# Storing a second MLP's weights already split, spacing that work out, and starting the second MLP inside the last block of the first

## The chip, the cores and the metric

The kernel runs on one NeuronCore of one Trainium2 chip. The metric is device time in microseconds, the median of three runs. Besides it there is one profiled execution, from which every number of the trace comes. The engines are PE (matrix products), ACT, DVE and POOL (elementwise work) and SP, which here only issues DMA transfers. Each engine takes its instructions strictly in order.

## The reference

Three stages follow each other, all in float32 with inputs given as float64:

- attention over 4 batches, 8 heads, 768 positions and 64 features, in which a query sees the keys less than 16 positions away and 24 block summaries (the maximum of 32 keys, the mean of 32 values);
- a first MLP on the 3072 tokens of 512 features: `h = max(max(x @ w1, x @ w2), x @ w3)` with 768 hidden features, then `h @ w_out`;
- a second MLP with 2048 hidden features: `h = x @ w_in`, `g = h * tanh(softplus(h))`, `out = g @ w_out`.

## The kernel before

**Products.** A float32 operand is held as two parts, high (`..h`, rounded to the type that PE multiplies in one pass) and low (`..l`, the rest). Each product is three matmuls: high by high, high by low, low by high. [...]

**First MLP and attention.** The tokens are 48 tiles of 64, in 8 blocks of 6 tiles (384 tokens). A block has 22 groups of matmuls: for each of six slices `f` of the hidden features three groups of 12 (`gemm1`: `one`, `two_`, `three`, weight slots `a{f}`, `a{f}`, `b{f//2}`), then four groups of 18 (`gemm2`, slots `c{f//2}`). After `one` ACT copies the product to `m` (L532), after `two_` and `three` DVE takes the maximum into `m` (L536, L540), then ACT makes `hh` (L543) and DVE `hl` (L544). `gemm2` sums over all six `hh`, `hl`; ACT copies the sum to `y` (L562) and SP stores `y` to a buffer in HBM, `x2d`. `m` and `y` have one buffer each. The attention steps of later tiles (`attend`) are put between the groups.

**Weight jobs.** Weights come as float64 words. A job loads 512 KB (`fetch`), ACT takes the absolute value into `wa` (L163, two buffers of `wa`), and DVE makes the float32 value in six instructions (`narrow`, L171 to L184). `run_job` moves this pipeline on by a stage. The first 24 jobs are the first MLP's weights, among the attention of the start. The 32 `later_jobs` are the second MLP's: 16 slices of `w_in` and 16 of `w_out`, each stored to HBM as float32 by `keep` (L250). In the program they are called in blocks 2 and up, every third group; but the order on each engine is set by a scheduler that puts an instruction where its own model finds the engine free, so a call's place is no bound.

**Loading the second MLP's weights.** `load_b` (L260 to L265) loads a slice's two parts of 256 KB into a staging tile `wl` (two buffers), ACT makes the high parts (L189), POOL subtracts for the low parts (L190), each over 128x1024. The first six slices go into slots `a0` to `a5`, as block 7 of the first MLP leaves them; the next ten go into `b`, `c` and four extra tiles `wx`, one at each of the first ten steps of the second MLP.

**Second MLP.** 8 blocks of 384 tokens by 16 slices are 128 steps. A step is 12 matmuls of 384 columns into a PSUM tile `up` (`g3`), the activation on ACT and DVE (`mish_a`, `mish_b`, `mish_c`: `e`, `ep`, `n`, `r`, `p`, `u`, `g`, `gh`, `gl`), and, three steps later (`LAG`), 9 matmuls of 512 columns into the accumulators (`g4`). `up` shares four PSUM banks (`gps`) with the products of the first MLP, and a bank is free when DVE has read it for `p` (L643). All of this is written behind the last group of block 7.

Of the kernel before, what the change touches and what calls it, by code (L numbers as in the profile page):

```python
# [3 lines left out]

# [6 lines left out]
F32 = mybir.dt.float32  # L11
F32R = mybir.dt.float32r
U32 = mybir.dt.uint32
AF = mybir.ActivationFunctionType
ALU = mybir.AluOpType
# [4 lines left out]
P = 128  # L20
D = 64
QT = 64
# [8 lines left out]
AB = 2  # L31
# [3 lines left out]
BT = 6  # L35
PER = [1, 0, 1, 0, 0]
AHEAD = 5
JOBN = 3
JOB0 = 2
# [15 lines left out]
def tile_kernel(ctx, tc, q, k, v, w1, w2, w3, w_out, w_in2, w_out2, out):  # L55
    nc = tc.nc
# [6 lines left out]
    KC = DM // P  # L63
    NF1 = DF1 // P
    NF2 = DF2 // P
# [10 lines left out]
    NBLK = len(sizes)  # L76
    MAXT = max(sizes)
# [5 lines left out]
    dpool = ctx.enter_context(tc.tile_pool(name="dpool", bufs=1, space=DRAM))  # L83
# [20 lines left out]
    for kind in ("mid", "first", "last"):  # L104
        m = const.tile([P, KX], F32, name=f"mask_{kind}")
        nc.gpsimd.memset(m[:, 0:NB], math.log(BLK))
        nc.gpsimd.memset(m[:, NB:KX], 0.0)
        for lo in (0, QT):
# [3 lines left out]
                out=r, in_=r, compare_op=ALU.is_ge, fill=NEG,  # L112
# [3 lines left out]
                out=r, in_=r, compare_op=ALU.is_ge, fill=NEG,  # L116
# [8 lines left out]
    agem = ExitStack()  # L125
# [3 lines left out]
    att = ExitStack()  # L129
# [11 lines left out]
    def wslot(tag):  # L141
        return wpool.tile([P, 4, 512], F32R, name=tag, tag=tag)
# [17 lines left out]
    def size_of(words):  # L160
        hi = words.rearrange("p (n t) -> p n t", t=2)[:, :, 1]
        a = stage.tile([P, 512], F32, name="wa", tag="wa", bufs=AB)
        nc.scalar.activation(out=a, in_=hi.bitcast(F32), func=AF.Abs)  # L163
        return a
# [19 lines left out]
        nc.vector.tensor_tensor(out=a, in0=w, in1=a, op=ALU.add)  # L184
        return a, None

    def split(w, h, l):

        nc.scalar.copy(h, w)  # L189
        nc.gpsimd.tensor_tensor(out=l, in0=w, in1=h.bitcast(F32), op=ALU.subtract)  # L190

    fetched, sized, narrowed = [], [], []

    def run_job():

        if narrowed:
            w, rest, done = narrowed.pop(0)
            done(w, rest)
        if jobs:
            src, done, parts = jobs.pop(0)  # L200
            fetched.append((fetch(src), done, parts))
        if sized:
            words, a, done, parts = sized.pop(0)
            narrowed.append((*narrow(words, a, parts), done))
        if fetched and (len(fetched) > 1 or not jobs):
            words, done, parts = fetched.pop(0)
            sized.append((words, size_of(words), done, parts))

    def busy():
        return bool(jobs or fetched or sized or narrowed)  # L210

    jobs = []
# [30 lines left out]
    slots = [f"{n}{i}" for n, m in (("a", NF1), ("b", NF1 // 2), ("c", NF1 // 2)) for i in range(m)]  # L243
    later_jobs = []

    w2d = {f: dpool.tile([P, 2, 512], F32, name=f"w2d{f}") for f in range(NF2)}

    def keep(f, i):
        def done(w, _):
            nc.sync.dma_start(out=w2d[f][:, i], in_=w)  # L250

        return done

# [5 lines left out]

    def load_b(f, tl):  # L260
        wb[f] = tl
        w = sec["t"].tile([P, 2, 512], F32, name="wl", tag="wl")
        nc.sync.dma_start(out=w, in_=w2d[f])
        h, l = (tl.rearrange("p (c u) n -> p c u n", u=2)[:, :, u] for u in range(2))
        split(w, h, l)  # L265


    kTd = [dpool.tile([P, NP, S], F32, name=f"kTd{b}") for b in range(B)]
# [239 lines left out]


    hhl = {}  # L510

    def gemm1(i, f):

        n = sizes[i] * QT
        xh, xl = xhl[i]
        ps = []

        def product(which):
            w, part = wa[which, f]
            pt = gps.tile([P, 512], F32, name="hp", tag="g")  # L520
            ps.append(pt)
            for c in range(KC):
                wh, wl = w[:, part, c * P : (c + 1) * P], w[:, part + 1, c * P : (c + 1) * P]
                nc.tensor.matmul(pt[:, :n], lhsT=wh, rhs=xh[:, c, :n], start=(c == 0), stop=False)  # L524
                nc.tensor.matmul(pt[:, :n], lhsT=wh, rhs=xl[:, c, :n], start=False, stop=False)  # L525
                nc.tensor.matmul(pt[:, :n], lhsT=wl, rhs=xh[:, c, :n], start=False, stop=(c == KC - 1))  # L526

        m = g2.tile([P, MAXT * QT], F32, name="m", tag="m")

        def one():  # L530
            product(1)
            nc.scalar.copy(m[:, :n], ps[0][:, :n])  # L532

        def two_():
            product(2)
            nc.vector.tensor_tensor(out=m[:, :n], in0=ps[1][:, :n], in1=m[:, :n], op=ALU.max)  # L536

        def three():
            product(3)
            nc.vector.tensor_tensor(out=m[:, :n], in0=ps[2][:, :n], in1=m[:, :n], op=ALU.max)  # L540
            hh = gx.tile([P, MAXT * QT], F32R, name=f"hh{f}", tag=f"hh{f}")
            hl = gx.tile([P, MAXT * QT], F32R, name=f"hl{f}", tag=f"hl{f}")
            nc.scalar.copy(hh[:, :n], m[:, :n])  # L543
            nc.vector.tensor_tensor(out=hl[:, :n], in0=m[:, :n], in1=hh[:, :n].bitcast(F32), op=ALU.subtract)  # L544
            hhl[i, f] = (hh, hl)

        return [one, two_, three]

    def gemm2(i, e):
        n = sizes[i] * QT  # L550

        def emit():
            pt = gps.tile([P, 512], F32, name="yp", tag="g")
            for f in range(NF1):
                w, part = wa[4, f]
                hh, hl = hhl[i, f]
                wh, wl = w[:, part, e * P : (e + 1) * P], w[:, part + 1, e * P : (e + 1) * P]
                nc.tensor.matmul(pt[:, :n], lhsT=wh, rhs=hh[:, :n], start=(f == 0), stop=False)  # L558
                nc.tensor.matmul(pt[:, :n], lhsT=wh, rhs=hl[:, :n], start=False, stop=False)  # L559
                nc.tensor.matmul(pt[:, :n], lhsT=wl, rhs=hh[:, :n], start=False, stop=(f == NF1 - 1))  # L560
            y = g2.tile([P, MAXT * QT], F32, name="y", tag="y")
            nc.scalar.copy(y[:, :n], pt[:, :n])  # L562
            nc.sync.dma_start(out=x2d[i][:, e, :], in_=y[:, :n])

        return [emit]
# [7 lines left out]
    def open_second():  # L573
        sec["stack"] = ExitStack()
        pool = lambda name, bufs: sec["stack"].enter_context(tc.tile_pool(name=name, bufs=bufs, side="right"))
        sec["x"] = {0: pool("bx", 1)}
        sec["g"] = pool("bg", 4)
        sec["t"] = pool("bt", 2)
        sec["t1"] = pool("bt1", 1)
        sec["ps"] = sec["stack"].enter_context(tc.tile_pool(name="bps", bufs=1, space=PSUM))  # L580
# [143 lines left out]
    def attend(upto):  # L724
        nonlocal nstep
        while nstep < min(upto, len(steps)):
            steps[nstep]()
            nstep += 1
# [4 lines left out]
            run_job()  # L733
        nit += 1

    second_open = False
    for i in range(NBLK):
        groups = []
        for f in range(NF1):
            groups += [(f, g) for g in gemm1(i, f)]  # L740
        for e in range(KC):
            groups += [(None, g) for g in gemm2(i, e)]
        G = len(groups)
        for n_, (f, g) in enumerate(groups):
            if i == JOB0 and n_ == 0:
                jobs.extend(later_jobs)
            if busy() and (i < JOB0 or n_ % JOBN == 0):
                run_job()
            g()
            attend(4 * BT * (i + 1) + (4 * BT * (n_ + 1)) // G + (AHEAD * min(n_ + 1, 8)) // 8)  # L750
            if i == NBLK - 1 and f is not None and n_ % 3 == 2:
                if not second_open:
                    att.close()
                    open_second()
                    second_open = True
                    for c in range(KC):
                        load_x2(0, c)()
                load_b(f, wslot(slots[f]))
    agem.close()
    wx = ctx.enter_context(tc.tile_pool(name="wx", bufs=1))  # L760
    extra = [wx.tile([P, 4, 512], F32R, name=f"wx{j}") for j in range(NF2 - 2 * NF1)]
    sec["x"][1] = ctx.enter_context(tc.tile_pool(name="bx1", bufs=1))
    later = [(f, (lambda f=f: wslot(slots[f])) if f < 2 * NF1 else (lambda f=f: extra[f - 2 * NF1]))
             for f in range(NF1, NF2)]

    seq = [(i, f) for i in range(NBLK2) for f in range(NF2)]
    LAG = 3
    for s in range(len(seq) + LAG):
        if s < len(seq):
            i, f = seq[s]  # L770
            if i + 1 < NBLK2 and f >= 6 and f % 2 == 0:
                if f > 6:
                    x2n()
                if f < 6 + 2 * KC:
                    x2n = load_x2(i + 1, (f - 6) // 2)
            if i == 0 and later:
                fl, mk = later.pop(0)
                load_b(fl, mk())
        if 2 <= s < len(seq) + 2:
            mish_c(seq[s - 2])  # L780
        if s < len(seq):
            g3(i, f)
            mish_a(seq[s])
        if 1 <= s < len(seq) + 1:
            mish_b(seq[s - 1])
        if s >= LAG:
            g4(seq[s - LAG])
    sec["stack"].close()


# [25 lines left out]
```

## Time and profile before

| | us |
|---|---|
| median of 3 runs | 1156.06 (1150.07 to 1156.34) |
| profiled execution, its own time | 1153.23 |
| its span, first to last instruction | 1151.5 |
| PE busy in the span | 1115.4 (97%) |
| PE weight loads | 1015.8 (88%) |
| DVE busy | 831.7 (72%) |
| ACT busy | 556.0 (48%) |
| POOL busy | 122.0 (11%) |

The mean granted clock of PE is 0.993 of full speed. The span has three stages: to about 90 us the start (attention, first weights), to about 605 us the rest of attention with the first MLP, then the second MLP. PE is the engine with most work, so its idle time, and what ended each wait, is the first thing to read; the share of another engine matters only in a stretch where PE waited for it.

### The profile page before, as it was taken

What the parts mean: (1) busy time and instruction counts of PE and PEld (TensorE: products, weight loads), DVE (VectorE), ACT (ScalarE), POOL (GpSimd) and SP (SyncE); (2) the same over time, 40 slices, a digit from 0 to 9 for tenths busy, and PEclk for the clock granted to TensorE, in tenths of its full rate; (3) what the DMA queues carried; (4) which work ended last, traced back from release to release, by engine and by line L of the source; (5) the groups of instructions that cost most, each with busy time, mean ns of one, the idle gap of its engine ahead of it and who ended that gap; (6) DMA issues with size and microseconds to landing.
All of it is one profiled execution on the core that took longest, in us unless ns stands there. A gap on an engine that the chain in (4) does not pass through costs nothing.

```text
span 1151.5 us, 18165 instructions
## 1 busy us (share of the span) xinstructions
PE 1115.4 (97%) x6656; PEld 1015.8 (88%) x6656; DVE 831.7 (72%) x1734; ACT 556.0 (48%) x1375; POOL 122.0 (11%) x155
## 2 busy tenths in 40 slices
PE   7789999999999999999997999999999999999998
PEld 4548989989999999999996899999989899999997
DVE  4789998989983534332219987887877888787776
ACT  5676554444453433332335554554545455454543
POOL 3000111311032101100255000000000000000000
PEclk9989999999999999999998999999999999999999
DMA  9997578897865321112244010100101010010000
GB/s 254 249 237 201 147 192 239 236 243 204 252 158 136 77 73 39 46 32 71 90 131 126 1 56 1 28 28 2 54 1 55 1 28 28 5 38 1 28 1 27
DMA packets 181100, 109.86 MB, mean 95 GB/s; under 512 B 129556, under 2 KB 167444, under 8 KB 181012
## 3 DMA queue, kind: packets, MB, share of 16 engines
q1 hardware_dynamic: 181012, 108.72, 34.6%
q8 instruction: 52, 0.85, 0.3%
q14 instruction: 36, 0.29, 0.1%
HBM read 81.28 MB, written 27.41 MB: 94 GB/s over the span
## 4 chain that ended last, share of the span: by engine, by line
PE 78%; DVE 9%; issue 5%; DMA 3%; POOL 2%; ACT 2%; ACTq 0%; POOLq 0%; DVEq 0%; SPq 0%
PE acc L670 8%; PE acc L671 8%; PE acc L672 8%; PE up L615 8%; PE up L617 8%; PE up L616 7%; PE hp L524 6%; PE hp L526 6%; PE hp L525 6%; PE sc L405 3%; DMA w2d<-wa 2%; PE yp L558 2%; PE xp L451 2%; PE yp L559 2%; PE yp L560 2%
## 5 line engine op out<-in xcount | busy, mean ns | idle before, releaser
L633 ACT ACTIVATE r<-n,two 128x384 f32<-128x384 f32 x128 | 78.9, 617 | 153.3 <-DVE n L630 153.2
L524 PE MATMUL hp<-xh,a 128*128 128x384 f32 x384 | 134.0, 349 | 1.5 <-ACT y L562 1.5
L526 PE MATMUL hp<-xh,a 128*128 128x384 f32 x384 | 129.1, 336 | 0.0
L525 PE MATMUL hp<-xl,a 128*128 128x384 f32 x384 | 128.9, 336 | 0.0
L656 DVE TENSOR_TENSOR gl<-g,gh 128x384 fp32r<-128x384 f32 x128 | 71.3, 557 | 61.9 <-ACT gh L655 61.3
L626 ACT ACTIVATE e<-up 128x384 f32<-128x384 f32 x128 | 62.7, 490 | 85.1 <-PE up L617 84.6
L420 ACT ACTIVATE s<-s,nm 128x120 f32<-128x120 f32 x168 | 64.3, 385 | 40.0 <-DVE nm L417 38.6
L628 DVE TENSOR_SCALAR ep<-e 128x384 f32<-128x384 f32 x128 | 47.3, 370 | 43.6 <-ACT e L626 43.4
L524 PEld LDWEIGHTS hp<-xh,a 128*128 128x128 f32 x384 | 72.3, 188 | 3.6 <-ACT y L562 2.2
L630 DVE SCALAR_TENSOR_TENSOR n<-e,ep 128x384 f32<-128x384 f32 x128 | 74.5, 582 | 0.3
L648 DVE SCALAR_TENSOR_TENSOR g<-u,n 128x384 f32<-128x384 f32 x128 | 73.0, 570 | 0.8
L646 DVE SCALAR_TENSOR_TENSOR u<-u,p 128x384 f32<-128x384 f32 x128 | 72.8, 569 | 0.2
L525 PEld LDWEIGHTS hp<-xl,a 128*128 128x128 f32 x384 | 72.3, 188 | 0.4 <-issue 0.3
L615 PE MATMUL up<-x2h,a 128*128 128x384 f32 x192 | 65.7, 342 | 7.1 <-DVE p L643 7.1
L643 DVE TENSOR_TENSOR p<-up,r 128x384 f32<-128x384 f32 x128 | 70.6, 552 | 2.6 <-ACT r L634 2.2
L655 ACT CAST gh<-g 128x384 fp32r<-128x384 f32 x128 | 64.2, 502 | 17.0 <-DVE g L648 17.0
L526 PEld LDWEIGHTS hp<-xh,a 128*128 128x128 f32 x384 | 72.1, 188 | 0.1
L645 DVE SCALAR_TENSOR_TENSOR u<-n,r 128x384 f32<-128x384 f32 x128 | 70.3, 549 | 0.0
L524 PE MATMUL hp<-xh,b 128*128 128x384 f32 x192 | 68.0, 354 | 0.0
L634 ACT ACTIVATE r<-r 128x384 f32<-128x384 f32 x128 | 67.0, 523 | 0.8
L558 PE MATMUL yp<-hh,c 128*128 128x384 f32 x192 | 65.9, 349 | 1.3 <-ACT hh L543 1.2
L617 PE MATMUL up<-x2h,a 128*128 128x384 f32 x192 | 65.5, 341 | 0.0
(175 smaller groups left out, 3030.2 us busy)
## 6 DMA issues: line engine op xcount, KB each, us to landing
words<-in_moe_w_out SPq DMA_DIRECT2D x22, 512.0 KB, 3.9
words<-in_moe_w SPq DMA_DIRECT2D x18, 512.0 KB, 5.1
words<-in_moe_w_in SPq DMA_DIRECT2D x16, 512.0 KB, 4.6
w2d<-wa SPq DMA_DIRECT2D x32, 256.0 KB, 2.8
wl<-w2d SPq DMA_DIRECT2D x16, 512.0 KB, 3.5
vr<-in_v SPq DMA_DIRECT2D x40, 192.0 KB, 2.9
kT<-kTd SPq DMA_DIRECT2D x38, 192.0 KB, 4.3
nat<-in_q SPq DMA_DIRECT2D x24, 256.0 KB, 3.1
```

The costliest lines, as they stand in the source:

```text
L524: nc.tensor.matmul(pt[:, :n], lhsT=wh, rhs=xh[:, c, :n], start=(c == 0), stop=False)
L525: nc.tensor.matmul(pt[:, :n], lhsT=wh, rhs=xl[:, c, :n], start=False, stop=False)
L526: nc.tensor.matmul(pt[:, :n], lhsT=wl, rhs=xh[:, c, :n], start=False, stop=(c == KC - 1))
L558: nc.tensor.matmul(pt[:, :n], lhsT=wh, rhs=hh[:, :n], start=(f == 0), stop=False)
L615: nc.tensor.matmul(pt[:, :N2], lhsT=wh, rhs=xh[:, c], start=(c == 0), stop=False)
L616: nc.tensor.matmul(pt[:, :N2], lhsT=wh, rhs=xl[:, c], start=False, stop=False)
L617: nc.tensor.matmul(pt[:, :N2], lhsT=wl, rhs=xh[:, c], start=False, stop=(c == KC - 1))
L630: nc.vector.scalar_tensor_tensor(out=n, in0=e, scalar=E20, in1=e2, op0=ALU.min, op1=ALU.mult)
L633: nc.scalar.activation(out=r, in_=d["n"], func=AF.Ln, bias=two[:, 0:1])
L670: nc.tensor.matmul(o, lhsT=gh[:, c], rhs=w[:, 2], start=(f == 0), stop=False)
L671: nc.tensor.matmul(o, lhsT=gh[:, c], rhs=w[:, 3], start=False, stop=False)
L672: nc.tensor.matmul(o, lhsT=gl[:, c], rhs=w[:, 2], start=False, stop=(f == NF2 - 1))
```

## The change

- `keep` now splits a weight slice as it is stored: ACT copies the high part into `wr` (two buffers), DVE subtracts in place in `wa`, and two transfers of 256 KB go out instead of one. The HBM tile of a slice has four parts instead of two.
- `load_b` loads the four parts straight into the slot. The staging tile, the ACT copies and the POOL subtractions are gone; a load is 1 MB instead of 512 KB.
- From block 2 on, `size_of` of a job (L163) is ordered on ACT behind the last ACT instruction that the groups before it issued (`last["act"]`), so it can't be drawn forward.
- `m` and `y` share one pair of buffers (`my`).
- The body of the second MLP's loop is a function, `second_step`, and its first three steps are issued behind the first three `gemm2` groups of block 7.

```diff
-    def split(w, h, l):
-
-        nc.scalar.copy(h, w)
-        nc.gpsimd.tensor_tensor(out=l, in0=w, in1=h.bitcast(F32), op=ALU.subtract)
-
-    def run_job():
+    def run_job(after=None):
...
-            sized.append((words, size_of(words), done, parts))
+            with tc.issue_after(after) if after else nullcontext():
+                a = size_of(words)
+            sized.append((words, a, done, parts))
...
-    w2d = {f: dpool.tile([P, 2, 512], F32, name=f"w2d{f}") for f in range(NF2)}
+    w2d = {f: dpool.tile([P, 4, 512], F32, name=f"w2d{f}") for f in range(NF2)}
 
     def keep(f, i):
         def done(w, _):
-            nc.sync.dma_start(out=w2d[f][:, i], in_=w)
+            h = stage.tile([P, 512], F32R, name="wr", tag="wr", bufs=AB)
+            nc.scalar.copy(h, w)
+            nc.vector.tensor_tensor(out=w, in0=w, in1=h.bitcast(F32), op=ALU.subtract)
+            nc.sync.dma_start(out=w2d[f][:, 2 * i], in_=h.bitcast(F32))
+            nc.sync.dma_start(out=w2d[f][:, 2 * i + 1], in_=w)
...
     def load_b(f, tl):
         wb[f] = tl
-        w = sec["t"].tile([P, 2, 512], F32, name="wl", tag="wl")
-        nc.sync.dma_start(out=w, in_=w2d[f])
-        h, l = (tl.rearrange("p (c u) n -> p c u n", u=2)[:, :, u] for u in range(2))
-        split(w, h, l)
+        nc.sync.dma_start(out=tl.bitcast(F32), in_=w2d[f])
...
-        m = g2.tile([P, MAXT * QT], F32, name="m", tag="m")
+        m = g2.tile([P, MAXT * QT], F32, name="m", tag="my", bufs=2)
...
-            nc.scalar.copy(m[:, :n], ps[0][:, :n])
+            last["act"] = nc.scalar.copy(m[:, :n], ps[0][:, :n])
...
-            y = g2.tile([P, MAXT * QT], F32, name="y", tag="y")
-            nc.scalar.copy(y[:, :n], pt[:, :n])
+            y = g2.tile([P, MAXT * QT], F32, name="y", tag="my", bufs=2)
+            last["act"] = nc.scalar.copy(y[:, :n], pt[:, :n])
...
             if busy() and (i < JOB0 or n_ % JOBN == 0):
-                run_job()
+                run_job(last["act"].ins if i >= JOB0 else None)
             g()
...
                 load_b(f, wslot(slots[f]))
+            if i == NBLK - 1 and f is None and early < LAG:
+                second_step(early)
+                early += 1
     agem.close()
...
-    for s in range(len(seq) + LAG):
+    for s in range(early, len(seq) + LAG):
+        second_step(s)
```

**What the change moves on ACT.** The first place is ACT at the end of block 2 and the first two slices of block 3. `y` and `m` are the copies of the first MLP, `wa<-words` opens a later job. Before (block 2's last `y` first):

```order
L562 COPY y<-yp 128x384
L163 ACTIVATE wa<-words 128x512
L532 COPY m<-hp 128x384
L420 ACTIVATE s,esum<-s,nm 128x120 x4
L163 ACTIVATE wa<-words 128x512
L543 CAST hh_3338<-m 128x384
L532 COPY m<-hp 128x384
L163 ACTIVATE wa<-words 128x512
L440 COPY pT<-ptp 120x512
L460 CAST xh<-xp 128x4x64
L163 ACTIVATE wa<-words 128x512
L543 CAST hh_3416<-m 128x384
```

Now, from block 2's last `y` on as well:

```order
L561 COPY y<-yp 128x384
L163 ACTIVATE wa<-words 128x512
L458 CAST xh<-xp 128x4x64
L248 CAST wr<-wa 128x512
L531 COPY m<-hp 128x384
L418 ACTIVATE s,esum<-s,nm 128x120 x4
L248 CAST wr<-wa 128x512
L542 CAST hh_3362<-m 128x384
L163 ACTIVATE wa<-words 128x512
L531 COPY m<-hp 128x384
L438 COPY pT<-ptp 120x512
L458 CAST xh<-xp 128x4x64
```

Before, 26 of the 32 later jobs were opened ahead of block 2's last `y`, 13 of them ahead of block 1's, and the last one in block 3's third slice. Now none stands ahead of block 2: they are opened eight to a block in blocks 2 to 5, about one to a slice and two among `gemm2`, each with one `wr` copy behind it.

**What it moves on PE.** The second place is PE between block 7's `gemm2` (`yp`) and the second MLP (`up`, `acc`). Before, the last rows of `gemm2` and the first of `g3`; six steps of `g3`, 72 matmuls, stand ahead of the first `acc`:

```order
L558 MATMUL yp<-hh_6412,c_1467 128x384
L559 MATMUL yp<-hl_6413,c_1467 128x384
L560 MATMUL yp<-hh_6412,c_1467 128x384
L615 MATMUL up<-x2h,a_6161 128x384
L616 MATMUL up<-x2l,a_6161 128x384
```

Now `g3` of step 0 stands inside the first group of `gemm2`, ahead of its last slice:

```order
L557 MATMUL yp<-hh_6477,c_1467 128x384
L558 MATMUL yp<-hl_6478,c_1467 128x384
L559 MATMUL yp<-hh_6477,c_1467 128x384
L614 MATMUL up<-x2h,a_6289 128x384
L615 MATMUL up<-x2l,a_6289 128x384
L616 MATMUL up<-x2h,a_6289 128x384
```

Step 1 follows the second group, step 2 the third, step 3 the fourth, and the first `acc` comes behind step 3, after 48 `up` matmuls with 57 of `gemm2` among them.

## Rows read from the trace of the kernel before

**Rows 1.** Stretches: us, busy of PE, PEld, DVE, ACT, POOL, granted clock, DMA share, GB/s.

```profile
0.00:90.00 90.00, 71.06 (x418) 45.35 (x419) 62.67 (x135) 57.86 (x164) 9.47 (x46) 0.94 1.02 244
150.00:360.00 210.00, 204.39 (x1473) 195.56 (x1473) 186.26 (x385) 97.51 (x296) 46.47 (x61) 1.00 0.78 215
360.00:600.00 240.00, 240.00 (x1663) 233.76 (x1662) 83.80 (x170) 84.04 (x243) 40.96 (x34) 1.00 0.25 70
600.00:630.00 30.00, 22.91 (x112) 21.44 (x111) 23.37 (x31) 16.88 (x31) 16.90 (x6) 0.89 0.48 151
630.00:1140.00 510.00, 510.00 (x2554) 460.23 (x2553) 413.92 (x887) 260.96 (x537) 2.40 (x1) 1.00 0.06 20
```

**Rows 2.** PE's waits from 150 to 360 us: total, times, longest, us.

```profile
PE ptp L438 <- POOL s L431: 2.6, 2, 1.5
PE hp L524 <- ACT y L562: 1.5, 2, 1.2
PE yp L558 <- ACT hh L543: 1.2, 1, 1.2
```

**Rows 3.** PE's waits from 600 to 660 us.

```profile
PE up L615 <- DVE p L643: 7.1, 2, 6.1
```

**Rows 4.** The chain that ended last, 600 to 630 us: start, us, what.

```profile
603.54 0.93 ACT c L189
...
604.99 0.40 ACT e L626
...
618.44 0.69 PE up L615
...
624.97 0.18 PE up L615
```

**Rows 5.** Timeline, 605 to 617 us, of DVE: start, us, instruction, shape.

```profile
613.43 2.69 DVE L646 SCALAR_TENSOR_TENSOR u<-u,p 128x384 f32<-128x384 f32 x1
```

**Rows 6.** Timeline of POOL in the same stretch.

```profile
613.05 2.65 POOL L190 TENSOR_TENSOR wx<-wl,wx 128x1024 fp32r<-128x1024 f32 x1
```

**Rows 7.** The same line of DVE, 660 to 1140 us: count, busy us, mean ns, idle.

```profile
L646 DVE SCALAR_TENSOR_TENSOR u<-u,p 128x384 f32<-128x384 f32 x115 | 63.5, 552 | 0.2
```

**Rows 8.** Timeline of PE in the second MLP: two steps' first matmuls.

```profile
922.42 0.34 PE L615 MATMUL up<-x2h,wx 128*128 128x384 f32 x1
...
926.59 0.34 PE L615 MATMUL up<-x2h,wx 128*128 128x384 f32 x1
```

**Rows 9.** Stretches: with later jobs, block 5 without, block 7.

```profile
300.00:330.00 30.00, 29.82 (x223) 28.44 (x222) 29.46 (x60) 14.99 (x47) 5.93 (x8) 1.00 0.74 204
...
427.60:491.90 64.30, 64.30 (x468) 62.18 (x469) 25.20 (x54) 24.21 (x82) 6.12 (x6) 1.00 0.20 50
...
556.30:605.10 48.80, 48.80 (x283) 48.80 (x283) 12.39 (x18) 18.84 (x28) 24.73 (x11) 1.00 0.36 114
```

**Rows 10.** DVE's job lines, 150 to 540 us, columns as in rows 7.

```profile
L184 DVE TENSOR_TENSOR wa<-words,wa 128x512 f32<-128x512 f32 x34 | 26.8, 787 | 0.1
L181 DVE SCALAR_TENSOR_TENSOR wa<-words,wa 128x512 f32<-128x512 uint32 x33 | 23.7, 719 | 0.4
L176 DVE SCALAR_TENSOR_TENSOR words<-words,wa 128x512 uint32<-128x512 uint32 x33 | 22.9, 695 | 0.5
...
L179 DVE TENSOR_SCALAR wa<-words 128x512 uint32<-128x512 uint32 x33 | 15.7, 475 | 0.4
L171 DVE TENSOR_SCALAR wa<-wa 128x512 f32<-128x512 f32 x33 | 15.3, 463 | 4.0 <-ACT wa L163 3.7
...
L173 DVE TENSOR_SCALAR wa<-wa 128x512 uint32<-128x512 uint32 x33 | 14.7, 446 | 0.3
```

**Rows 11.** DVE's L184 over the span: duration ns min/median/max, first and last start.

```profile
L184 DVE TENSOR_TENSOR wa<-words,wa x42: 675/685/1477, 99.5 to 329.6; 128x512 f32<-128x512 f32 x42
```

**Rows 12.** POOL's costliest group, 150 to 660 us, columns as in rows 7.

```profile
L431 POOL TENSOR_TENSOR s<-s,rs 128x480 f32<-128x480 f32 x34 | 36.0, 1060 | 214.7 <-DVE rs L429 166.4 <-ACT qT L364 30.4 <-PE ptp L438 8.6
```

**Rows 13.** Loads of a slice (L263, 512 KB), from issue to landing.

```profile
DMA to landing us min/median/max: 3.4/3.5/4.1
```

## What the change will do to the time

> **What bounds the kernel now.** I read the stretches first [rows 1]. The reader is to see that PE is busy for every microsecond of 360 to 600 and of 630 to 1140, at full granted clock, so nothing can be won there: its matmuls are the same after the change. Time is lost in three places: the start (71.06 us busy of 90), 150 to 360 (204.39 of 210) and 600 to 630 (22.91 of 30, clock 0.89). The change leaves the start alone. So the prediction is about the other two.
>
> Then PE's waits in these two. From 150 to 360 us it waits 2.6 us for POOL's normalisation, 1.5 for ACT's `y` copy, 1.2 for `hh` [rows 2]. From 600 to 660 us there is a single cause: 7.1 us, in two waits, for DVE's `p`, which frees a bank of `up` [rows 3].
>
> The chain of waits tells why `p` is late [rows 4]. ACT finishes the copy of a `c` slice (L189) before it comes to `e` of the second MLP at 604.99, and PE's next `up` starts at 618.44. In between DVE crawls: an instruction that takes 552 ns on average in the rest of the second MLP [rows 7] takes 2.69 us from 613.43 [rows 5], and it ends 0.4 us after POOL's subtraction of 2.65 us [rows 6]. So the seam is made by the three jobs of `load_b`: a transfer that ACT's queue waits on, ACT's copy, and POOL's subtraction, which DVE stands still for. PE has run five steps of `g3` into four banks by then and can't go on.
>
> **The change, part by part.**
>
> *The seam.* Removed are 16 copies on ACT and 16 subtractions on POOL, and the first three steps begin ahead of the seam. PE then has the remaining groups of `gemm2` between the steps, so a bank is wanted again only after 18 matmuls of `gemm2` and 12 of `g3`. The idle 7.1 us go [rows 3]. The wait also costs clock: the step that starts at 618.44 ends at 624.97 [rows 4], 6.53 us, while a step takes 926.59 - 922.42 = 4.17 [rows 8], so 2.4 us more were lost: after the 6.1 us of idling PE ran for a while at 1.2 instead of 2.4 GHz, which is the 0.89 of the 30 us [rows 1]. Sum 9.5 us. Late next could be the first `acc`, which needs `gl` of step 0; between step 0's `g3` and it stand 57 matmuls of `gemm2` and 36 of `g3`, 93 at the pace of 21 in a step of 4.17 us, over 15 us, against about 6 us of activation (seven DVE and four ACT instructions of some 0.5 us). I take all 9.5; the bounds are 7.1 (only the idle time) and 9.5.
>
> *The loads.* A load of 512 KB lands in 3.5 us [rows 13]; one of 1 MB is not in the trace, so its bounds are 3.5 and twice that, 7.0. I take a value near the lower half: in block 7 the DMA engines are busy for 0.36 of the time at 114 GB/s [rows 9], 5.6 MB in 48.8 us, and 4.5 to 5 MB more bring that to about 0.65, still below 1. Nine slices are issued through block 7 and seven at its end; a slice is used every 4.17 us and the last seven are not wanted before step 9. Cost nothing; the cover is that lead.
>
> *The jobs.* Each of 32 jobs gains an ACT copy, a DVE subtraction and a second store. ACT is busy for 97.51 of 210 us in the stretch where it opens the later jobs now [rows 1]; 32 copies of at most 0.7 us over four blocks are hidden there. DVE is the engine to watch. A job's six instructions are 787 + 719 + 695 + 475 + 463 + 446 ns = 3.6 us [rows 10], the subtraction has the shape of the first and gets its 0.8, together 4.4. Eight jobs in a block are 35 us. A block without jobs has 25.2 us of DVE work in 64.3 [rows 9]. The sum, 60 of 64.3, is 94%. That is about what DVE has now in the stretch with jobs: 29.46 of 30 us at the worst, where PE still lost only 0.18 us [rows 9]. So the jobs take four blocks at the load that they now impose on 170 us.
>
> What PE lost there was 5.3 us [rows 2], and each wait costs PE a little more to refill; with 0.2 us for each of five that is 6.3. The 1.5 us behind `y` go: a `y` copy waited for the store of the one before, now there are two buffers. The other 3.8 are DVE's queue. I expect no change of kind: one delay of `hh` or of the normalisation per loaded block, four blocks at some 0.7 us, 2.8 us. So 6.3 - 2.8 = 3.5 us are won. The bounds: 6.3 (no wait is left), and a loss of 5.3 (twice today's waits, because the load lasts longer).
>
> A rule speaks against moving the subtraction to DVE. The trace shows first how much of it there is: the like instruction L184 takes 675 ns at least and 1477 at most, 685 in the median [rows 11], so few of 42 met something, and the mean of 787 that I use holds it. The Trainium skill, SBUF — State Buffer, in its summary of rules, says that a DVE instruction with two SBUF inputs and a GpSimd instruction that reads SBUF exclude each other for a whole instruction. The rows of the seam agree with it (2.69 us beside 2.65). By that rule alone, if each subtraction met a normalisation, it is the second rival; by the rows the price is 0.1 us a job and is in the sum.
>
> *Sum.* 9.5 + 3.5 = 13.0 us. The profiled execution took 1153.2, its span 1151.5; less 13 that is **1140**. The median of the runs, 1156.06, is 2.8 above the profiled execution and the lowest run 3.1 below it, so I leave the number as it stands. Against that median it is 1.4% less.
>
> **The rivals.**
>
> 1. *The jobs win nothing.* DVE at 94% over four blocks instead of in a burst brings PE's waits back, up to the bound: 1153.2 - 9.5 + 0 to 5.3 = 1144 to 1149. For it: all the waits but the one for `y` come from a loaded DVE, and the load lasts longer. Against it: 300 to 330 us, fuller still, and 0.18 lost. Chance 0.23.
>
> 2. *DVE becomes the bound of blocks 2 to 5 (slower).* Place: the new subtraction beside POOL's normalisation, 34 of 1.06 us each [rows 12]. If each of eight jobs of a block stood still for one, DVE's block grows by 8.5 us to 68.5, and with the 3% that DVE idles even when full, 2 us a block, to 70.5: 6.2 over the block's 64.3, four times, 25 us. Time 1153.2 - 9.5 + 25 = 1169. It decides once DVE's work and its own idle time in a block pass 64.3, that is, 4 us above the sum. Against it is the median of L184. The rule of the skill named above is what would bring it. Chance 0.05.
>
> 3. *The seam comes back as a wait for weights.* If 1 MB takes 7.0 us and the loads go one after another, 16 take 112 us; the first can start some 8 us into block 7, at 564, and the last lands at 676, while step 15 comes 12 steps of 4.17 after about 607, at 657: 19 us of waits, 1153.2 - 13 + 19 = 1159. Against it is the DMA share of 0.36 [rows 9], which leaves room for loads that overlap. Chance 0.04.
>
> 4. *The change doesn't do what it says.* The order shows that it does: the jobs stand eight to a block and the steps stand inside `gemm2`. No chance is kept for it.
>
> **How the numbers follow.** My forecast has 0.68, the rivals 0.23, 0.05 and 0.04. The likeliest case alone spans 1153.2 - 15.8 = 1137 to 1144, and the runs scatter by 3 us on either side, so the range starts at 1134. It reaches to 1151 and so takes in the first rival with that scatter; it leaves out the second and third and some tail. A measurement of this kernel can tell 1% from no change; 1% below 1156.06 is 1144.5. Faster by over 1% is most of the forecast and a small part of the first rival, 0.66; within 1% 0.29; slower by over 1% is the second rival, 0.05.
>
> **What would show it.** The seam: PE's waits after block 7 should hold no `up` behind `p` of more than 1 us, the granted clock should stay at 1.00 there, and a DVE instruction of 0.55 us should keep that. The jobs: L163 from about 235 to 495 us, eight to a block; DVE 90 to 95% busy in blocks 2 to 5; PE's waits there 3 us in all, none for `y`. The loads: no PE wait for a slot. I am wrong if waits for `hh` or the normalisation pass 6 us, if PE waits for a weight slice, or if blocks 2 to 5 grow beyond 64.3 us.

## The result, and the profile after

The changed kernel takes 1138.94 us (median of 4 runs, 1136.94 to 1139.87), the kernel before 1155.12 (4 runs, 1150.07 to 1156.34). The ratio is 0.9864, 95% interval 0.9840 to 0.9888. Forecast were 1140 and 1134 to 1151. The profiled execution took 1139.57 us (span 1137.6), 13.7 less than that of before; the sum in the prediction was 13.0.

The stretches of the kernel after, columns as in [rows 1]:

```profile
0.00:90.00 90.00, 70.24 (x413) 44.62 (x413) 61.92 (x133) 56.73 (x162) 9.49 (x46) 0.92 1.01 240
150.00:360.00 210.00, 210.00 (x1528) 202.55 (x1527) 149.69 (x304) 99.80 (x304) 47.15 (x64) 1.00 0.63 175
360.00:600.00 240.00, 238.62 (x1638) 232.36 (x1637) 149.43 (x301) 95.10 (x274) 20.45 (x21) 1.00 0.52 160
600.00:630.00 30.00, 30.00 (x156) 27.62 (x155) 23.06 (x49) 15.39 (x32) 0.00 (x0) 1.00 0.71 278
```

PE has the same 6656 matmuls in both traces, so only its lost time can change. Against [rows 1] the reader is to see three things. From 150 to 360 us PE is now busy throughout, and DVE's work there has fallen from 186 to 150 us; what was moved stands in the next stretch together with new subtractions, 149 in place of 84. From 600 to 630 us PE has 30.00 us in place of 22.91, at full clock, and POOL nothing. The start lost a little (clock 0.92 in place of 0.94), though its code is the same.

In place of the five waits of [rows 2], 5.3 us together, PE has a single one between 100 and 600 us, and from 600 to 660 us, where [rows 3] has 7.1 us, none:

```profile
PE yp L557 <- ACT hh L542: 1.4, 1, 1.4
```

DVE's `u` (now L645), which took 2.69 us in [rows 5], keeps its 0.55 us in all of its 128 instructions, those at the seam (the passage from block 7's `gemm2` to the second MLP) included. The line's duration in ns, min/median/max, first and last start:

```profile
L645 DVE SCALAR_TENSOR_TENSOR u<-u,p x128: 547/551/559, 592.7 to 1129.0; 128x384 f32<-128x384 f32 x128
```

The later jobs are opened (L163) from 234.0 to 487.8 us, as forecast. The job's lines on DVE and ACT from 220 to 500 us, columns as in [rows 7], with the new subtraction (L249) and the new copy (L248):

```profile
L184 DVE TENSOR_TENSOR wa<-words,wa 128x512 f32<-128x512 f32 x32 | 24.8, 775 | 0.7
L249 DVE TENSOR_TENSOR wa<-wa,wr 128x512 f32<-128x512 f32 x32 | 22.4, 700 | 2.9 <-ACT wr L248 2.6
...
L163 ACT ACTIVATE wa<-words 128x512 f32<-128x512 f32 x32 | 21.5, 672 | 3.6 <-DMA w2d<-wa 3.6
L248 ACT CAST wr<-wa 128x512 fp32r<-128x512 f32 x32 | 19.8, 620 | 46.5 <-DVE wa L184 40.4 <-DMA kT<-kTd 3.3 <-issue 2.8
```

ACT stood 40.4 us behind L184 before its new copies: its queue is in order, and the copy stands in it ahead of the next `hh` or `y`. That is a wait the prediction didn't list; it has a part in the 1.4 us that PE still waits (below).

To compare stages I add up, over all of PE's matmuls, the time from one start to the next beyond the median of that shape in the kernel before. By this sum PE lost 9.3 us between 100 us and the seam and 10.7 from the seam on before, 4.1 and 0.7 after. Some 0.7 from the seam on, and about 1.6 ahead of it (the least that any kernel here shows, e4), are many small steps and no waits. The table has these two sums for every kernel, each from one profiled execution; "jobs" is the first, "seam" the second. A ratio is to the kernel before as it was timed together with that run: 1155.12 us for the change, 1155.22 for e1 to e4, 1154.96 for e5 to e8, 1154.55 for e9 to e12.

| kernel | median us (range) | ratio to before (95%) | jobs | seam |
|---|---|---|---|---|
| before | 1155.12 | 1 | 9.3 | 10.7 |
| after | 1138.94 | 0.9864 (0.9840 to 0.9888) | 4.1 | 0.7 |
| e1, no early steps | 1137.25 (1136.88 to 1139.66) | 0.9855 (0.9832 to 0.9879) | 4.3 | 0.7 |
| e2, early steps alone | 1149.26 (1146.33 to 1154.71) | 0.9957 (0.9939 to 0.9976) | 11.7 | 8.0 |
| e3, no spacing | 1144.77 (1144.21 to 1145.14) | 0.9921 (0.9902 to 0.9941) | 12.9 | 0.7 |
| e4, spacing alone | 1145.02 (1143.22 to 1145.56) | 0.9921 (0.9900 to 0.9942) | 1.6 | 10.8 |
| e5, DVE for POOL at the seam | 1156.40 (1154.87 to 1159.80) | 1.0013 (0.9999 to 1.0028) | 13.2 | 13.8 |
| e6, one buffer | 1139.24 (1136.14 to 1141.77) | 0.9865 (0.9839 to 0.9892) | 5.4 | 0.7 |
| e7, not stored split | 1143.82 (1143.49 to 1144.32) | 0.9907 (0.9892 to 0.9922) | 2.6 | 6.3 |
| e8, POOL subtracts in the jobs | 1138.42 (1136.59 to 1140.14) | 0.9857 (0.9838 to 0.9877) | 4.6 | 0.7 |
| e9, POOL beside the loads | 1146.73 (1146.35 to 1148.48) | 0.9945 (0.9927 to 0.9963) | 3.6 | 12.0 |
| e10, ACT beside the loads | 1139.01 (1136.24 to 1139.77) | 0.9869 (0.9851 to 0.9888) | 3.8 | 0.8 |
| e11, six jobs a block | 1135.97 (1134.03 to 1138.21) | 0.9848 (0.9829 to 0.9867) | 2.4 | 0.7 |
| e12, stored split alone | 1151.65 (1149.78 to 1155.60) | 0.9981 (0.9969 to 0.9993) | 16.4 | 1.1 |

How far one execution can be trusted shows in kernels that are the same program up to block 7. Before, e2 and e5 have the same instructions in the same order on every engine there, and lose 9.3, 11.7 and 13.2 us; after, e1, e9 and e10 lose 4.1, 4.3, 3.6 and 3.8. So bunched jobs lose more, and a difference of up to 4 us between two kernels with bunched jobs shows nothing.

### The profile page after: what moved, and what is told of

It is laid out like the page before. It is cut to its first block, busy times and chain, and to the rows that moved or that the text cites. A ratio compares the mean times of both kernels' runs of the same rounds, so it can differ in the third digit from the quotient of the medians.

```text
span 1137.6 us, 18286 instructions
## 1 busy us (share of the span) xinstructions
PE 1112.0 (98%) x6656; PEld 1014.3 (89%) x6656; DVE 842.4 (74%) x1766; ACT 558.1 (49%) x1391; POOL 83.0 (7%) x139
## 4 chain that ended last, share of the span: by engine, by line
PE 63%; DVE 2%; ACT 1%; issue 1%; DMA 0%; SPq 0%; ACTq 0%
PE up L616 8%; PE up L614 8%; PE acc L669 8%; PE up L615 8%; PE acc L670 8%; PE acc L671 8%; PE hp L523 3%; PE hp L525 3%; PE hp L524 3%; PE yp L557 1%; PE yp L559 1%; PE yp L558 1%; PE sc L403 1%; PE xp L449 1%; PE ptp L436 0%
## 5 line engine op out<-in xcount | busy, mean ns | idle before, releaser
L418 ACT ACTIVATE s<-s,nm 128x120 f32<-128x120 f32 x168 | 64.3, 385 | 33.1 <-DVE nm L415 32.3
L645 DVE SCALAR_TENSOR_TENSOR u<-u,p 128x384 f32<-128x384 f32 x128 | 70.6, 552 | 0.4
L629 DVE SCALAR_TENSOR_TENSOR n<-e,ep 128x384 f32<-128x384 f32 x128 | 70.6, 552 | 0.3
```

## Experiments: which part of the change does what

**e1: the change without its early steps.**

```diff
-            if i == NBLK - 1 and f is None and early < LAG:
+            if False:
```

> The change without its early steps: weights stored split, jobs spaced, two output buffers, but the second MLP begins behind block 7's last product, with six steps of g3 ahead of the first acc. If the seam was made by load_b's copies and subtractions, their absence alone is enough: DVE's instructions take 0.55 us, p of step 0 comes some 5 us after its g3, the four banks last 8.3 us, and PE waits 0 to 1 us there, 1139 to 1140 us. If the lead of the early steps was what closed the seam, most of the 9.5 us is back: 1146 to 1149.

The seam stays closed with all 72 matmuls of `g3` ahead of the first `acc`, as in the kernel before, and the time is that of the change. The early steps contribute nothing beside the other parts.

**e2: the early steps alone,** on the kernel before (`second_step` and its call in block 7, nothing else).

```diff
+            if i == NBLK - 1 and f is None and early < LAG:
+                second_step(early)
+                early += 1
...
+    for s in range(early, len(seq) + LAG):
+        second_step(s)
```

> The kernel before with the early steps alone: old loads with ACT copies and POOL subtractions, jobs drawn forward, one buffer each for m and y. If load_b's work makes the seam, DVE still stands still beside POOL and some 2 to 4 us of the 9.5 stay: about 1148 to 1149. If the lead alone closes it, all 9.5 go: 1145 to 1146. The waits from 150 to 360 us stay near 5.3 in both.

The lead hides part of the wait and moves the rest. The median is some 6 us below that of before; the trace, which is of the slowest of the ten runs (1154.71 us), has a seam of 8.0 in place of 10.7. PE's waits from 100 to 660 us in e2 have, in place of [rows 3], the first `acc` waiting for the activation:

```profile
PE acc L673 <- ACT gh L658: 4.2, 2, 3.5
PE ptp L440 <- POOL s L433: 2.8, 2, 2.0
```

So the activation behind the seam is still late, and PE now meets it at the first `acc`.

**e3: the change without the order on ACT.**

```diff
-                run_job(last["act"].ins if i >= JOB0 else None)
+                run_job()
```

> The change without the order on the jobs: the scheduler may draw them forward into blocks 0 to 4. If the burst of jobs on DVE made PE's waits from 150 to 360 us, 2.5 to 4 us of them come back and the time is 1142 to 1143, with all of the seam still won. If the second buffer for m and y did it, the time stays at 1139.

The jobs bunch again, one subtraction larger: DVE is busy for 187.63 of the 210 us from 150 to 360, where the change has 149.69. PE's waits from 100 to 660 us:

```profile
PE yp L557 <- ACT hh L542: 4.5, 3, 2.9
PE ptp L436 <- POOL s L429: 1.9, 2, 1.2
```

Spacing is worth about 6 us beside the other parts, more than the 2.5 to 4 expected.

**e4: the order on ACT alone,** on the kernel before (`after` in `run_job`, `last["act"]`; one buffer each for `m` and `y`, no stored split, no early steps).

```diff
+            with tc.issue_after(after) if after else nullcontext():
+                a = size_of(words)
...
+                run_job(last["act"].ins if i >= JOB0 else None)
```

> The kernel before with the order on the jobs alone (weights stored as before, old loads, one buffer each, no early steps). If spacing wins the 3.5 to 5 us of the stage with jobs, 1150 to 1152, with the seam's 7.1 us of waits untouched. If the buffers win them, 1154 to 1156, and y's waits remain.

Of the waits from 100 to 660 us one line is left, the seam's; those for the normalisation, for `hh` and, with one buffer, for `y` are gone:

```profile
PE up L618 <- DVE p L646: 7.1, 3, 6.1
```

The stage lost 7.7 us less than in the trace of before; by the medians spacing alone wins 10, where 3.5 to 5 were expected. The trace of before has the least loss of three executions of the same program (9.3, 11.7, 13.2), which is room for the rest. The loss of 1.6 is also less than the changed kernel's 4.1; that its jobs have no split to make is a likely reason and not shown by itself.

**e12: storing split alone,** on the kernel before.

```diff
+            nc.scalar.copy(h, w)
+            nc.vector.tensor_tensor(out=w, in0=w, in1=h.bitcast(F32), op=ALU.subtract)
...
-        split(w, h, l)
+        nc.sync.dma_start(out=tl.bitcast(F32), in_=w2d[f])
```

> The kernel before with one part of the change: weights stored split and loaded as four parts; jobs where the scheduler draws them, one buffer, no early steps. Theory: the seam is closed by storing split alone, so its 9.9 us are won, and the jobs, one DVE subtraction larger in the same 170 us, lose 10 to 13 in place of 9.3 (as without spacing in e3, 12.9): 1155 - 9.9 + 1 to 4 = 1146 to 1149. Rival: the seam needs the early steps when the jobs end early: 1153 to 1156.

The seam closes without early steps, so the first theory's mechanism holds; its number does not: 1151.65 lies in neither range, because the bunched jobs lose 16.4 us in this trace and not 10 to 13. The stretches 150 to 360 and 600 to 630 us of e12:

```profile
150.00:360.00 210.00, 200.74 (x1432) 190.81 (x1431) 186.69 (x379) 106.33 (x305) 44.31 (x57) 0.99 0.81 229
600.00:630.00 30.00, 29.92 (x164) 28.41 (x163) 16.32 (x37) 14.00 (x29) 0.00 (x0) 1.00 0.71 280
```

DVE was already at 186 of 210 us before [rows 1] and does no more there now, nor in e3 (187.63); the work lasts longer, and PE falls from 204.39 to 200.74. By medians, storing split alone wins 3 us, spacing alone 10, both together (e1, and two buffers) 18. That is 5 more than the sum of the two, which fits split work that costs little only where the jobs are spaced.

**e7: the change with the old split** (float32 stored; staging tile, ACT copy and POOL subtraction at the load).

```diff
-        nc.sync.dma_start(out=tl.bitcast(F32), in_=w2d[f])
+        w = sec["t"].tile([P, 2, 512], F32, name="wl", tag="wl")
+        nc.sync.dma_start(out=w, in_=w2d[f])
...
+        split(w, h, l)
```

> The change without storing the weights split: spaced jobs, two buffers and early steps, but load_b copies on ACT and subtracts on POOL as before. It shows what storing them split is worth beside the early steps: 2 to 4 us if load_b's work makes the seam (1141 to 1143), nothing if the lead alone closes it (1138 to 1139, a little less since the jobs have a subtraction less on DVE).

Here the early steps hide part: no `up` waits for `p` any more, `acc` waits for `gh` (3.8 us in three waits) and once for `gl` (0.6). Its seam is 6.3, that of e4, which loads in the same way without early steps, 10.8. Five us are lost against the change. Storing split is what closes the seam.

**e6: one buffer each for `m` and `y`; e8: the new subtraction of the jobs on POOL.**

```diff
-        m = g2.tile([P, MAXT * QT], F32, name="m", tag="my", bufs=2)
+        m = g2.tile([P, MAXT * QT], F32, name="m", tag="m")
...
-            y = g2.tile([P, MAXT * QT], F32, name="y", tag="my", bufs=2)
+            y = g2.tile([P, MAXT * QT], F32, name="y", tag="y")
```

> The change with one buffer each for m and y. If the second buffer removed the wait behind y's store, about 1.5 us of waits for ACT's y copy come back at the ends of blocks: 1140 to 1141. If the spaced jobs make the stores land early enough, none comes back: 1139.

```diff
-            nc.vector.tensor_tensor(out=w, in0=w, in1=h.bitcast(F32), op=ALU.subtract)
+            nc.gpsimd.tensor_tensor(out=w, in0=w, in1=h.bitcast(F32), op=ALU.subtract)
```

> The change with the jobs' subtraction on POOL instead of DVE. DVE has 22 us less to do in blocks 2 to 5, POOL 32 instructions of 128x512 more, for each of which DVE can stand still. If DVE's load is what remains of PE's waits (1.4 us), they go and the time is 1137 to 1139; if the two engines shutting each other out costs more, waits of 2 to 5 us come and it is 1141 to 1144.

Both take the time of the change within their scatter. e6 has one wait of 0.4 us for `y`, where [rows 2] had 1.5: once the jobs are spaced, the store of a `y` lands in time but for that, and the second buffer wins nothing that the times can show. Its trace has 2.2 us of waits for `hh` and loses 5.4 in the stage, a little more than the change. In e8 the wait of 1.4 us for `hh` is left as in the change, with one of 0.2 for `hl`; which engine subtracts does not show among spaced jobs.

## Experiments: what makes the seam

The prediction named three jobs of `load_b` at once. These runs part them.

**e5: the kernel before with the subtraction at the load on DVE.**

```diff
-        nc.gpsimd.tensor_tensor(out=l, in0=w, in1=h.bitcast(F32), op=ALU.subtract)
+        nc.vector.tensor_tensor(out=l, in0=w, in1=h.bitcast(F32), op=ALU.subtract)
```

> The kernel before with load_b's subtraction on DVE instead of POOL; nothing else is changed. It parts the two causes at the seam. If DVE standing still beside POOL was the larger one, PE's wait for p falls from 7.1 to 2 to 4 us, though DVE has 16 more instructions of about 1.3 us: 1149 to 1152. If ACT's copies and the transfers ahead of them were the larger one, the wait stays at 6 to 8 us: 1154 to 1157.

Nothing is won. By its number the second theory, ACT's copies and the transfers, would stand, but the run does not settle it, since it trades one wait for others. PE's waits from 600 to 660 us, then ACT's from 590:

```profile
PE up L615 <- DVE p L643: 3.7, 1, 3.7
PE up L615 <- ACT y L562: 3.4, 1, 3.4
```

```profile
ACT y L562 <- DMA x2d<-y: 7.0, 1, 7.0
```

The last `y` copy waits for the store of the one before, and that store stands on SP's queue behind loads that wait for a staging tile, which DVE now frees late.

**e9 and e10: e1 with one suspect added back by itself.** The loads bring the split weights straight into the slots; behind each of the 16 loads stands one instruction whose result goes to a scratch tile that nothing reads.

```diff
+        d = sec["t1"].tile([P, 2, 512], F32, name="dm", tag="dm")
...
+        nc.gpsimd.tensor_tensor(out=d, in0=l.bitcast(F32), in1=h.bitcast(F32), op=ALU.subtract)
```

> The kernel of e1_no_early (1137.3) with a POOL subtraction of 128x1024 added behind each load of a slice; its result goes to a scratch tile that nothing reads. Theory A, DVE standing still for POOL makes the seam: the waits of up for p come back, 3 to 6 us and the clock with them, time 1141 to 1147. Theory B, ACT's copies behind the transfers make it: no wait above 1 us at the seam, although single DVE instructions there take over 2 us, time 1137 to 1139.

```diff
+        d = sec["t1"].tile([P, 2, 512], F32R, name="dm", tag="dm")
...
+        nc.scalar.copy(d, h.bitcast(F32))
```

> The kernel of e1_no_early (1137.3) with an ACT copy of 128x1024 added behind each load, which waits for the transfer; its result goes to a scratch tile that nothing reads. Theory A (POOL): no wait above 1 us at the seam, 1137 to 1139. Theory B (ACT waits in order for each transfer, and the activation stands behind it): the waits of up for p or for e come back, 3 to 7 us, time 1141 to 1147. If both e9 and e10 stay at 1137 to 1139, only the two together, or the staging tile between them, make the seam.

These two show what each does by itself. With ACT's copies there is no wait at the seam, with POOL's subtractions it is back, somewhat larger than before. The stretch 600 to 630 us, e10 first, then e9, and PE's waits of e9 from 590 to 680 us:

```profile
600.00:630.00 30.00, 30.00 (x155) 27.45 (x155) 29.23 (x66) 23.65 (x45) 0.00 (x0) 1.00 0.50 201
```

```profile
600.00:630.00 30.00, 21.41 (x98) 19.18 (x98) 29.83 (x40) 11.67 (x25) 15.17 (x6) 0.83 0.43 176
```

```profile
PE up L617 <- DVE p L645: 8.6, 2, 8.0
```

DVE's count tells it: 66 instructions in 30 us beside ACT's copies, 40 beside POOL's subtractions, and busy all the time in both. The timeline of DVE in e9 (start, us, instruction), then POOL's:

```profile
597.59 2.36 DVE L630 TENSOR_SCALAR ep<-e 128x384 f32<-128x384 f32 x1 [1.12 <-ACT e L628]
599.87 0.55 DVE L645 TENSOR_TENSOR p<-up,r 128x384 f32<-128x384 f32 x1
600.34 2.30 DVE L632 SCALAR_TENSOR_TENSOR n<-e,ep 128x384 f32<-128x384 f32 x1
602.56 2.71 DVE L647 SCALAR_TENSOR_TENSOR u<-n,r 128x384 f32<-128x384 f32 x1
605.20 2.49 DVE L630 TENSOR_SCALAR ep<-e 128x384 f32<-128x384 f32 x1
607.61 0.55 DVE L648 SCALAR_TENSOR_TENSOR u<-u,p 128x384 f32<-128x384 f32 x1
608.18 2.58 DVE L650 SCALAR_TENSOR_TENSOR g<-u,n 128x384 f32<-128x384 f32 x1
...
616.45 0.35 DVE L630 TENSOR_SCALAR ep<-e 128x384 f32<-128x384 f32 x1
616.72 0.55 DVE L648 SCALAR_TENSOR_TENSOR u<-u,p 128x384 f32<-128x384 f32 x1
```

```profile
597.33 7.53 POOL L266 TENSOR_TENSOR dm<-c 128x1024 f32<-128x1024 f32 x3 [3.97 <-DMA c<-w2d]
604.94 2.53 POOL L266 TENSOR_TENSOR dm<-wx 128x1024 f32<-128x1024 f32 x1
607.63 8.01 POOL L266 TENSOR_TENSOR dm<-wx 128x1024 f32<-128x1024 f32 x3 [0.16 <-DMA wx<-w2d]
```

POOL's instructions follow each other almost without a gap, three in 7.53 us, and DVE gets one of its own through for each; L648 at 607.61 comes through in the one gap of 0.16 us, and from 615.98 on, with POOL done, the same lines take 0.35 and 0.55 us again. `p` (L645) at 599.87 reads PSUM for one input and takes 0.55 us in the middle of POOL's. Of the six instructions of a step from `ep` to `g` four are held, each for about 2 us, and PE waits at the end of that for `p`.

One thing of the kernel before is not in either run: the long waits for transfers. ACT's waits from 590 to 620 us, before and then e10:

```profile
ACT b L189 <- DMA wl<-w2d: 5.1, 2, 4.0
ACT c L189 <- DMA wl<-w2d: 4.8, 2, 3.9
```

```profile
ACT dm L266 <- DMA c<-w2d: 1.7, 1, 1.7
```

Before, the first `e` starts 4.4 us after the first `up` (600.48 and 604.88), behind such a wait; in e10 2.3 us after it (593.40 and 595.70). So e9 shows that POOL's subtractions are enough to make a seam of this size, and e10 that ACT's copies alone cost nothing. How the 10.0 us of the kernel before divide between POOL and the transfers that wait for a staging tile, no run shows.

## Experiment: the jobs spread further

The one wait left in the changed kernel is the same effect on a small scale. DVE at 409 us of the kernel after, then POOL:

```profile
408.76 0.69 DVE L181 SCALAR_TENSOR_TENSOR wa<-words,wa 128x512 f32<-128x512 uint32 x1
409.48 1.36 DVE L184 TENSOR_TENSOR wa<-words,wa 128x512 f32<-128x512 f32 x1
410.76 0.54 DVE L539 TENSOR_TENSOR m<-hp,m 128x384 f32<-128x384 f32 x1
```

```profile
408.98 1.32 POOL L429 TENSOR_TENSOR s<-s,rs 128x480 f32<-128x480 f32 x1 [10.28 <-DVE rs L427]
```

L184 is held by the normalisation, 0.67 us longer than usual; `m` comes late behind it and ends at 411.30; ACT takes its copy for the job (L248) and one of the attention first, and `hh` starts at 411.67, when PE has waited since 410.85. **e11** spreads the jobs further.

```diff
-JOBN = 3
-JOB0 = 2
+JOBN = 4
+JOB0 = 1
```

> The changed kernel with the later jobs from block 1 on, every fourth group in place of every third from block 2: six a block, over blocks 1 to 6. DVE's load in a block falls from 8 to 6 jobs (6 x 4.4 + 25 = 51 of 64 us). Theory: what is left of the loss among the jobs, 4.1 us, comes from jobs lying too close in one block; then 2 to 3 us are won, 1136 to 1137 beside 1138.9. Rival: it comes from single collisions that any spacing leaves, or from attention of block 1: no change, 1138 to 1140.

No wait of PE from 100 to 660 us is left in the trace, and the job stage loses 2.4 us in place of 4.1. That is below the 3.6 to 4.3 of the four kernels with the change's jobs. The median, 1135.97, is the lowest of all; but its interval (0.9829 to 0.9867) overlaps that of the change, so the gain over the change is shown for this stage in one trace, and not by the times.

## Why the prediction was right, step by step

- **The seam, 9.5 us.** Right in size: 10.7 lost before, 0.7 after, 10.0 won. Wrong in two of its reasons. "The seam is made by the three jobs of `load_b`" is shown for one of the three: POOL's subtraction brings back 11.3 us by itself (e9), ACT's copies nothing (e10). The wait for transfers was put back by no run, so its share stays open. I took these two from the chain [rows 4], where ACT's `c` copy stands ahead of `e`; the chain names who came last, not who was slow. And the early steps, which the step credits with keeping a bank free, win nothing (e1).
- **The first `acc` next.** Right for the change, which has no wait there. With POOL's subtractions left at the seam it is what waits, 3.5 us at most in e2 and 1.5 in e7.
- **The loads, nothing.** Right in cost, wrong in the bound of 7.0 us for 1 MB. The issues of the kernel after from 540 to 640 us, with KB and median us to landing:

```profile
a<-w2d SPq DMA_DIRECT2D x6, 1024.0 KB, 4.7
wx<-w2d SPq DMA_DIRECT2D x4, 1024.0 KB, 16.9
```

  The first six, spread over block 7, land in 4.7 us; the last four, issued with three others within 6 us, take 16.9. The lead still covers it, as the first `wx` is used at step 12.
- **The jobs, 3.5 us.** 5.2 were won (9.3 - 4.1). With the time that PE needs to refill, the five waits of before cost 6.1 us in its trace, which the prediction had at 6.3; the term that was mis-sized is the residual of 2.8, one wait of 1.4 us that costs 1.5. The other 0.6 are small steps. Two steps of this part failed. DVE was to be 94% busy in blocks 2 to 5. Measured from the last `y` of one block to that of the next, for blocks 2 to 5, columns as in [rows 1]:

```profile
225.10:289.90 64.80, 64.80 (x476) 62.65 (x476) 51.37 (x105) 31.56 (x96) 11.57 (x15) 1.00 0.66 181
289.90:356.50 66.60, 66.60 (x492) 64.41 (x494) 58.38 (x118) 35.05 (x103) 16.20 (x20) 1.00 0.82 228
356.50:423.10 66.60, 65.22 (x478) 62.74 (x479) 56.48 (x116) 32.65 (x100) 13.25 (x17) 1.00 0.71 210
423.10:487.50 64.40, 64.40 (x474) 62.28 (x474) 55.06 (x111) 32.91 (x99) 7.22 (x6) 1.00 0.59 172
```

  That is 79 to 88%; blocks 3 to 5 have eight L184 each, block 2's stretch six. Blocks 3 and 4 are longer than the 64.3 I had for each, but PE is busy in all of block 3's 66.6 us and in all but the one wait of block 4's, so the jobs did not stretch them. My sum added mean durations, but neighbours on DVE overlap: in the rows above L184 starts at 409.48 and lasts 1.36 us, to 410.84, and L539 starts at 410.76; in e9 L648 starts 0.27 us after an instruction of 0.35. Durations summed overstate a queue's load; the busy time of a stretch does not. The other failed step is the 1.5 us given to the second `y` buffer: the waits for `y` go with the spacing (e4, e6).
- **The start.** Left at nothing; the profiled execution lost 1.4 us more there than before. 10.0 + 5.2 - 1.4 = 13.8, against 13.7 measured.
- **Where luck had a part.** Between the medians the change wins 16.2 us and not 13.0. The trace that the sum was read from lost 9.3 us among the jobs, the least of the three executions of that program. The forecast set out from this execution, 1.9 us below the median, and took off 3.2 too little by the medians; the two errors offset each other in part, so that 1140 lies 1.1 from the measured median.
- **The rivals.** The jobs' gain is there (first rival). DVE did not become the bound (second): 683 ns is the median of the new subtraction and 1079 the longest of 32, so few met a normalisation. The rule of exclusion was weighed for the jobs, where it cost one wait; its price was at the seam, where the prediction saw DVE stand still for POOL but named it as one of three. PE waited for no weights (third).

The rule that I weighed, of the Trainium skill, SBUF — State Buffer, in its summary of rules, fits e9 line by line: instructions with two SBUF inputs that come beside POOL's are held for about as long as one of these takes, `p` with one input in PSUM is not. The same page of the Trainium skill, under Who interferes with whom, names `tensor_scalar` among the operations that can take the shared pair in a two-port mode; that fits `ep`, held at 2.36 and 2.49 us against 0.35.

## What to carry to other kernels

When an elementwise engine crawls at a place where its work is small, look for the engine whose instructions end when its own end, before looking at what the chain of waits names; then add that suspect by itself to a kernel without the wait, as e9 and e10 do. Moving such work into an earlier stage pays in full only if that stage has room on the engine that gets it (e12 against e1), and spacing it there costs no more than an order on one instruction. A lead given to a slow chain hides part of its delay and moves the place where the rest is met (e2, e7). And a stage's loss is worth reading in more than one execution before a sum is built on it: the same program lost 9.3 and 13.2 us.

## What the hardware showed beyond that

The start has the same code in all these kernels, yet by the sum used above PE loses up to 4 us more in the first 100 us of one trace than of another. The stretch 30 to 60 us of the kernels before, after, e10 and e11, in this order, columns as in [rows 1]:

```profile
30.00:60.00 30.00, 24.01 (x186) 17.70 (x186) 23.80 (x53) 20.11 (x63) 0.00 (x0) 0.94 1.08 242
```

```profile
30.00:60.00 30.00, 24.01 (x175) 17.81 (x175) 22.41 (x50) 18.91 (x60) 0.00 (x0) 0.89 1.06 243
```

```profile
30.00:60.00 30.00, 24.02 (x192) 17.29 (x191) 25.18 (x56) 20.79 (x64) 0.00 (x0) 1.00 1.09 247
```

```profile
30.00:60.00 30.00, 24.15 (x169) 18.22 (x167) 21.24 (x46) 17.70 (x57) 0.00 (x0) 0.83 1.01 229
```

PE is busy for the same 24 us, with pauses, and has done 192, 186, 175 or 169 matmuls by the granted clock: parts of the stretch ran at 1.2 and not 2.4 GHz. The four runs of the change go the same way: 1136.94 us at a mean clock of 0.996, 1138.31 at 0.995, 1139.57 and 1139.87 at 0.993. So 3 to 4 us of a difference between two of these kernels can be the start's, and parts worth less than that are told from the trace of their own stage. What makes the clock fall in one run and not in another stays open.
